# Remainder tiles moved to the beginning of a visit, and two pairs' loads moved to GpSimd's queue, in a fused cosine attention and two-layer MLP

## The chip, the cores and the metric

The kernel runs on one core of a Trainium2 chip. The metric is the device time of one execution in microseconds (us). The kernel before was run three times: 409.94 us in the median, 409.24 to 410.39. One more execution was profiled; it took 410.35 us, and its traced span is 408.6 us.

Engines are named as the profile names them: PE is TensorE (PEld its weight loads), DVE is VectorE, ACT is ScalarE, POOL is GpSimd, and SP is SyncE, which here only issues DMAs. DMAs issued by SP and those issued by GpSimd go through two different queues (q1 and q0 in the profile) to the same 16 DMA engines.

## The reference

Inputs are q, k and v, each 8 batches x 12 heads x 448 positions x 64 values in float32, tau = 0.1, and two weight matrices.

```
q_n = q / (norm(q, axis=-1) + 1e-6)
k_n = k / (norm(k, axis=-1) + 1e-6)
scores = q_n @ k_n.T / tau
attn = exp(scores - max) ; attn /= sum(attn) + 1e-9
x = (attn @ v) reordered to (8*448 tokens) x (12*64 = 768)
h = x @ w_in                  # 768 x 2048
g = max(0.01*h, h)
out = g @ w_out               # 2048 x 768
```

The output is 3584 x 768 in float32.

## The kernel before

**Units.** Two heads form a pair, so a batch has 6 pairs and the whole input 48 (numbered 0 to 47; pair s belongs to batch s // 6). The 448 positions are cut into three tiles of 128 and a remainder of 64. A pair's q and k lie in `raw_sb`, one of six slots (slot s % 6), so that loading pair s + 6 has to wait until pair s has been squared and normalised.

**Preparing a pair.** `load_qk(s)` (L134) issues four DMAs from SP: the main part of q, that of k, and the two remainders. `squares(s)` (L170) multiplies on GpSimd, `sums(s)` (L183) reduces on VectorE, `roots(s)` (L194) takes the square root on ScalarE as a logarithm and an exponential, `normalise(s)` (L210) adds the 1e-6, takes the reciprocal and multiplies q and k into `qn` on VectorE, and `transposes(s)` (L245) makes `qkT`, the transposed form. For the first ten pairs TensorE does the transposes and VectorE copies them out of PSUM; from pair 10 on (`DMA_FROM`) it is one transposing DMA issued from SP. `norm(s)` (L696) puts roots, normalise and transposes together, then issues the load of pair s + 4 (from pair 12 on; norm(11) loads 12 and 13), and then lets GpSimd square pair s + 2. Before it squares, GpSimd executes `hold`, a tiny copy that waits until `qn[s]` is written; all that GpSimd has after it waits too.

**Scores.** `key_tiles` (L264) takes a list of tiles. An ordinary tile (s, ki), ki from 0 to 2, is 128 keys of one pair against all 448 positions of both heads; a remainder tile (s, 3) holds the 64 remaining keys of two pairs, s - 1 and s, and so reads the transposed form of both. All matmuls of the list are issued first, each tile into two PSUM banks; then ScalarE takes the exponential of each tile. A batch has 18 ordinary tiles and 3 remainder tiles.

**Attend.** `attend_two` and `attend` (L656 to L683) sum the exponentials and multiply with v for four heads at a time (a j; three in a batch), ScalarE makes reciprocals of the sums, and `scale` on VectorE writes the result, transposed, to `xT`. `attend_batch(b)` does the three j of batch b. v and the weights are loaded by GpSimd's queue.

**The two layers.** Tokens are handled in eight chunks; chunk b has 384 tokens where b is even and 512 where it is odd, from the two batches of a pair of batches (batch 2m and 2m + 1). `firsts(b)` is layer one of chunk b: for 16 blocks m of 128 hidden columns, six matmuls each (kt = 0 to 5, 0.164 us apart with 384 columns), then the leaky ReLU on ScalarE. The first three blocks begin with kt 0 to 3 before kt 4 and 5 need the last attend's output. `groups` is layer two: for every 128 tokens 32 steps of two matmuls that run side by side, with the output row stored from SP.

**The order.** The order of work on each engine is written out by hand: an engine executes its instructions in the order of the program. One turn of the main loop is `visit(b)`, then `attend_batch(b + 1)`, then the loads of v for batch b + 2, then `firsts(b + 1)`. `visit(b)` (L725) is layer two of chunk b with the score tiles of batch b + 1 strewn in: the dictionaries `wide`, `three` and `four` say after which steps a tile comes, the first for all rows of 128 tokens but the last and the second for the last. Two remainder tiles come before the first step and the third after the last step. The argument `norms` hangs norm and sums calls on steps (row i, step n), and `between` in `firsts` hangs them on blocks m. Batches, chunks and visits are counted from 0.

**The beginning.** Pairs 0 to 5 are loaded at once by `load_first`, and their scores and attends run while the weights arrive. `bulk(s)` (L552) issues loads of v and w_in from GpSimd between pairs. Pairs 10 and 11 are loaded by SP behind explicit waits (`behind(...)`, L578 and L748). The four parts of w_out are loaded by GpSimd, the first after the third attend has written `xT` (L750 to L751) and the others in norm(6), norm(7) and norm(8). Visit 0 goes through two rows of 128 tokens at once in four parts, each part needing one of the four parts of w_out.

Of the kernel before, what the change touches and what calls it, by code (L numbers as in the profile page):

```python
# [16 lines left out]
def kernel(  # L17
# [37 lines left out]
    qtp = ctx.enter_context(tc.tile_pool(name="qt", bufs=5))  # L55
# [63 lines left out]
    def load_first(eng, x, part, s0, n):  # L119

        h0, i = 2 * s0, 0 if x is q else 1
        if part == 0:
            dst = raw_sb[:, s0 : s0 + n, :, 4 * i : 4 * i + 3]
            eng.dma_start(
                out=dst.rearrange("p s h t d -> p (s h) t d"), in_=main(x, 0, h0, 2 * n)
            )
        else:
            dst = raw_sb[64 * i : 64 * i + 64, s0 : s0 + n, :, 3]
            eng.dma_start(  # L129
                out=dst.rearrange("p s h d -> p (s h) d"),  # L130
                in_=x[0, h0 : h0 + 2 * n, MAIN:S].rearrange("h p d -> p h d"),
            )
# [340 lines left out]
    for part in range(2):  # L473
        load_first(nc.sync, q, part, 0, 1)
        load_first(nc.scalar, k, part, 0, 1)
    load_first(nc.sync, q, 0, 1, 1)
    load_first(nc.scalar, k, 0, 1, 1)
    for part, s, n in ((1, 1, 2), (0, 2, 1), (0, 3, 1), (0, 4, 1), (0, 5, 1)):
        for x in (q, k):
            load_first(nc.sync, x, part, s, n)  # L480
# [32 lines left out]
    for x in (q, k):  # L513
        load_first(gp, x, 1, 3, 3)
# [37 lines left out]
    def bulk(s):  # L552

        if s == 0:
            load_v(1)
            load_w_in(0, j=0)
        elif s == 1:
            load_v_rem(0, slice(2, 4))
            load_w_in(0, j=1)
        elif s == 2:  # L560
            load_w_in(0, j=2)
            load_v(2)
        elif s == 3:
            for e in range(2):
                load_w_in(1, e=e)

    def scaled(s):

        if s and s + 2 < NPAIR:
            sums(s + 2, (0,))  # L570
        normalise(s + 1)
        if s == 0:
            load_qk(7)
        elif s == 2:
            load_qk(8)
            load_qk(9)
        elif s == 4:
            behind(nc.sync, scalings[5], "weights first")  # L578
            load_qk(10)
        hold(qn[s + 1][:, 6, 0, 0:1])  # L580
        squares(s + 3)
        bulk(s)
        if s == 4:
            squares(8)
        if s + 2 < NPAIR:
            sums(s + 2, (1,))
# [67 lines left out]
    sums(8)  # L654
# [29 lines left out]

    def attend_batch(b):
        if b == 1:
            load_qk(14)
            load_qk(15)
            sums(12)
        attend_two(b * NQ)  # L690
        if b == 1:
            norm(12)
        attend(b * NQ + 2)


    def norm(s, transposed=True):  # L696
# [8 lines left out]
        for x in (12, 13) if s == 11 else (s + 4,) if s > 11 else ():  # L705
            load_qk(x)
# [18 lines left out]
    def visit(b, order, norms, between):  # L725
# [4 lines left out]
        key_tiles([(s0 + 1, 3), (s0 + 3, 3)])  # L730
        for i, pairs in enumerate(order):
            last = i == len(order) - 1
            after = between[last]
# [6 lines left out]
        key_tiles([(s0 + 5, 3)])  # L740

    three = ({5: 1, 11: 1, 16: 2, 21: 1, 27: 1}, {3: 1, 7: 1, 11: 1, 16: 2, 20: 1})
    wide = (dict.fromkeys((5, 11, 16, 22, 27, 33, 38, 44, 49, 55, 60), 1), {4: 1, 8: 1, 12: 1, 16: 2, 21: 1, 26: 1})
    four = ({5: 1, 11: 1, 16: 2, 24: 1}, {6: 1, 16: 2})
# [3 lines left out]
    behind(nc.sync, scalings[NQ - 1, 0], "weights first")  # L748
    load_qk(11)
    hold(xT[0][:, 2 * NQ - 2, 0:1])  # L750
    load_w_out((0,))  # L751
    norm(6, False)
    norm(7, False)
    firsts(
        0, SOON, {
            4: [lambda: norm(8, False)],
            5: [lambda: transposes(6), lambda: sums(9)],
            7: [lambda: transposes(7)],
            8: [lambda: norm(9, False)],
            10: [lambda: transposes(8), lambda: load_v(3)],  # L760
            11: [lambda: sums(10), lambda: load_v(4)],
            12: [lambda: transposes(9)],
            13: [lambda: norm(10), lambda: load_v(5), lambda: load_v_rem(1)],
# [3 lines left out]
    ready = 10  # L767
    for b in range(B):
# [9 lines left out]
        norms = {(0, 3): [lambda: norm(11)]}  # L778
        if b:
            norms = {}  # L780
            for i in range(tokens - 1):
                norms[i, 4] = [lambda s=ready + i: norm(s)]
                norms[i, 20] = [lambda s=ready + i + 1: sums(s)]
        visit(b, order, norms, wide if b == 0 else three if tokens == 3 else four)
        ready += tokens - 1
# [4 lines left out]
        s = ready  # L790
        between = {0: [lambda s=s: norm(s)], 1: [lambda s=s: sums(s + 1)]}
        if b == 0:
# [5 lines left out]
            ready += 4  # L798
        elif tokens == 3:
            between.update({  # L800
                4: [lambda s=s: norm(s + 1), lambda s=s: sums(s + 2)],
                7: [lambda s=s: norm(s + 2), lambda s=s: sums(s + 3)],
                10: [lambda s=s: norm(s + 3)], 13: [lambda s=s: sums(s + 4)],
            })
            ready += 4
        else:
            between.update({
                4: [lambda s=s: norm(s + 1)], 5: [lambda s=s: sums(s + 2)],
                8: [lambda s=s: norm(s + 2)], 12: [lambda s=s: sums(s + 3)],
            })  # L810
            ready += 3
# [36 lines left out]
```

## Time and profile before

| | us |
|---|---|
| median of three runs (lowest, highest) | 409.94 (409.24, 410.39) |
| the profiled execution | 410.35 |
| its span | 408.6 |
| TensorE matmul busy | 400.5 |
| ScalarE busy | 263.0 |
| VectorE busy | 189.8 |
| GpSimd busy | 139.7 |
| visit 0 begins | 52.1 |
| visit 2 begins | 147.4 |
| visit 4 begins | 242.1 |
| visit 6 begins | 336.8 |

A busy time is a sum over instructions; matmuls overlap and their ends are modelled, so a busy share of TensorE does not say that it runs at its peak. A timeline row gives the start and the length in us, the engine (SPq is SP's issuing of DMAs), the line, the operation with the tile written and the tile read, and how many instructions were merged; in brackets is the idle time of the engine before it and what ended that. A row of waits says who waited for whom: us in total, times, longest. Lines are those of the kernel before.

### The profile page before, as it was taken

How to read it: one execution, taken by the hardware profiler on the slowest of the kernel's cores; microseconds unless marked ns; L12 is line 12 of the kernel's file. 1: busy time of each engine (PE TensorE's matmuls, PEld its weight loads, DVE VectorE, ACT ScalarE, POOL GpSimd, SP SyncE). 2: the span in 40 equal slices, each digit the busy share in tenths (PEclk: the TensorE clock that was granted, in tenths of full speed). 3: DMA queues.
4: the chain of work that ended last, by engine and by line, in shares of the span. 5: the costliest groups of instructions: out<-in, count | busy, mean ns of one | idle time of the engine just before them, and what ended most of it. 6: DMA issues, size and time to landing. Idle time of an engine off the chain costs nothing.

```text
span 408.6 us, 10188 instructions
## 1 busy us (share of the span) xinstructions
PE 400.5 (98%) x4096; PEld 215.1 (53%) x4096; DVE 189.8 (46%) x405; ACT 263.0 (64%) x454; POOL 139.7 (34%) x214
## 2 busy tenths in 40 slices
PE   8998999999999999999999999999999999999996
PEld 3334556544555655544555555544555555544564
DVE  6887931761644724265552625257261645130021
ACT  5996488565866579745875569845776559944300
POOL 4983471481323433254241624055231530000000
PEclk9999999999999999999999999999999999999999
DMA  7999999697495939376386857486477732210033
GB/s 181 249 223 224 214 176 232 166 173 144 114 205 90 151 80 206 77 114 165 88 167 152 127 126 150 124 113 140 92 171 158 102 88 63 63 41 2 0 77 78
DMA packets 102111, 54.21 MB, mean 133 GB/s; under 512 B 70000, under 2 KB 97008, under 8 KB 102064
## 3 DMA queue, kind: packets, MB, share of 16 engines
q1 hardware_dynamic: 78064, 41.04, 43.6%
q0 software_dynamic: 23152, 12.00, 22.5%
q8 instruction: 32, 0.52, 0.5%
q10 hardware_dynamic: 848, 0.52, 0.4%
q14 instruction: 15, 0.12, 0.1%
HBM read 45.61 MB, written 11.01 MB: 139 GB/s over the span
## 4 chain that ended last, share of the span: by engine, by line
PE 86%; DMA 9%; POOL 2%; DVE 1%; issue 1%; ACT 0%; SPq 0%; POOLq 0%; DVEq 0%
PE ps L380 32%; PE ps L455 30%; PE ps L316 10%; PE ps L276 7%; DMA raw_sb<-in_k_dram 6%; PE ps L417 5%; DMA v_b<-in_v_dram 3%; POOL sq L179 1%; PE ps L303 1%; POOL v_rem L164 0%; DVE qn L219 0%; POOL w_in_sb L107 0%; POOL raw_sb L129 0%; ACT pe L288 0%; DVE xT L357 0%
## 5 line engine op out<-in xcount | busy, mean ns | idle before, releaser
L380 PE MATMUL ps<-xT,w_in_sb 128*128 128x384 bf16 (+1 forms) x768 | 147.9, 353 | 0.0
L455 PE MATMUL ps<-w_out_sb,hT 64*128 64x384 bf16 x1536 | 143.3, 323 | 0.0
L288 ACT ACTIVATE pe<-ps 128x896 bf16<-128x896 f32 x144 | 123.7, 918 | 19.8 <-PE ps L276 17.9
L387 ACT ACTIVATE hT<-ps 128x384 bf16<-128x384 f32 (+1 forms) x128 | 67.5, 543 | 72.7 <-PE ps L380 72.2
L380 PEld LDWEIGHTS <-w_in_sb 128*128 128x128 bf16 x768 | 74.0, 98 | 71.7 <-issue 3.7
L455 PEld LDWEIGHTS <-hT 64*128 64x128 bf16 x1536 | 74.9, 94 | 53.7 <-PE ps L455 4.0
L179 POOL TENSOR_TENSOR sq<-raw_sb 128x512 f32<-128x512 f32 x92 | 84.3, 936 | 21.1 <-DMA raw_sb<-in_k_dram 20.3
L219 DVE TENSOR_TENSOR qn<-raw_sb,r 128x512 bf16<-128x512 f32 x96 | 57.5, 640 | 1.6
L467 DVE COPY osb<-ps 128x384 f32<-128x384 f32 x41 | 21.2, 554 | 77.1 <-PE ps L455 46.6
L276 PE MATMUL ps<-qkT 64*128 64x448 bf16 (+1 forms) x384 | 54.7, 354 | 1.5 <-ACT pe L288 0.7
L190 DVE TENSOR_REDUCE ss<-sq 128x6 f32<-128x384 f32 (+1 forms) x95 | 54.4, 611 | 3.3 <-POOL sq L179 3.2
L510 POOL CAST seen<-qn 128x1 f32<-128x1 bf16 x47 | 8.9, 190 | 121.7 <-DVE qn L219 119.9
L214 DVE TENSOR_SCALAR ss<-ss 128x14 f32<-128x14 f32 x48 | 10.6, 222 | 66.2 <-ACT ss L198 66.2
L357 DVE TENSOR_TENSOR xT<-ps,rb 128x448 bf16<-128x448 f32 x48 | 27.9, 620 | 26.5 <-ACT rb L336 24.0
L157 POOL DMA_DIRECT2D v_b<-in_v_dram x24 | 18.5, 772 | 54.2 <-PE ps L316 54.2
L316 PE MATMUL ps<-pe,v_b 128*32 128x448 bf16 x576 | 32.0, 353 | 1.2 <-DMA v_b<-in_v_dram 1.2
L276 PEld LDWEIGHTS <-qkT 64*128 64x128 bf16 (+1 forms) x384 | 16.7, 96 | 21.1 <-issue 8.7
L316 PEld LDWEIGHTS <-v_b 128*32 128x32 bf16 x576 | 15.0, 97 | 13.4 <-DMA v_b<-in_v_dram 1.6
L423 DVE COPY osb<-ps 128x384 f32<-128x384 f32 (+1 forms) x9 | 4.6, 513 | 36.6 <-issue 22.6
L288 ACT ACTIVATE pr<-ps 128x896 bf16<-128x896 f32 x24 | 21.3, 921 | 0.2 <-PE ps L276 0.2
L335 ACT ACTIVATE rb<-ps 128x448 f32<-128x448 f32 x24 | 12.9, 538 | 13.2 <-PE ps L316 12.2
L417 PE MATMUL ps<-w_out_sb,hT 128*128 128x384 bf16 (+1 forms) x144 | 21.0, 308 | 0.0
(48 smaller groups left out, 186.5 us busy)
## 6 DMA issues: line engine op xcount, KB each, us to landing
raw_sb<-in_q_dram SPq DMA_DIRECT2D x48, 192.0 KB, 3.3
raw_sb<-in_k_dram SPq DMA_DIRECT2D x46, 192.0 KB, 3.4
out_dram<-osb SPq DMA_DIRECT2D x30, 192.0 KB, 2.9
v_b<-in_v_dram POOLq DMA_DIRECT2D x24, 192.0 KB, 4.9
out_dram<-osb SPq DMA_DIRECT2D x12, 384.0 KB, 2.9
w_out_sb<-in_moe_w_out_dram POOLq DMA_DIRECT2D x4, 768.0 KB, 10.4
w_in_sb<-in_moe_w_in_dram POOLq DMA_DIRECT2D x3, 512.0 KB, 9.3
w_in_sb<-in_moe_w_in_dram POOLq DMA_DIRECT2D x2, 768.0 KB, 15.2
```

Source lines behind the costliest of these rows:

```text
L179: eng.tensor_tensor(sq, x, x, op=ALU.mult)
L190: nc.vector.tensor_reduce(o.rearrange("p (h t) -> p h t", h=2), sqs[s][i], axis=AX.X, op=ALU.add)
L219: scalings[s] = nc.vector.tensor_tensor(qn[s][:, lo:hi], x.rearrange("p h t d -> p t h d"), r[:, r0 : r0 + 2 * nt].rearrange("p (h t) -> p ...
L276: nc.tensor.matmul(out=out[:, a, :S], lhsT=x[rows, c0:c1], rhs=x[rows, 0:S], start=True, stop=True,)
L288: nc.scalar.activation(out=dst, in_=sc[:, :, :S], func=AF.Exp, scale=inv_tau)
L316: nc.tensor.matmul(out=x[32 * g : 32 * g + 32, :S], lhsT=weights(g, ki) if ki < 3 else rem(g), rhs=pe[s][:, ki, a, :] if ki < 3 else pr[j] ...
L357: scalings[j, e] = nc.vector.tensor_tensor(xT[m][:, 2 * jj + e, half * S : (half + 1) * S], pos.pop((j, e))[:, :S], rbs[j], op=ALU.mult,)
L380: nc.tensor.matmul(out=pm[:, :n], lhsT=w_in_sb[:, kt, m * 128 : (m + 1) * 128], rhs=xT[c // 2][:, kt, c0 : c0 + n], start=(kt == 0), stop= ...
L387: nc.scalar.activation(out=hT[c][:, m, :n], in_=pms.pop((c, m))[:, :n], func=AF.Prelu, alpha=0.01)
L417: nc.tensor.matmul(out=po2[:, :n], lhsT=hT[c][:, m, ts * 128 : (ts + 1) * 128], rhs=w_out_sb[:, m, lo : lo + n], start=(m == 0), stop=(m = ...
L455: done[p][i] = nc.tensor.matmul(out=pos2[p][:, i, :HALF], lhsT=hT[c][rows, m, ts * 128 : (ts + 1) * 128], rhs=w_out_sb[rows, m, half * HAL ...
L467: copy(out=osb[c, ts][:, half * HALF : (half + 1) * HALF], in_=po2[:, i, :HALF])
```

## The change

There are five parts.

1. **Loads.** `load_first` becomes `load_pairs`, which can load several pairs of any batch. Pairs 10 and 11 are no longer loaded by SP behind waits; four DMAs on GpSimd's queue load both, issued in `scaled(4)` between squares(7) and squares(8), which puts them between the loads of w_in and those of w_out. The load of v for the third j comes ahead of the third w_in load in `bulk(2)`.
2. **Before visit 0.** roots(6) and normalise(6) come ahead of the third attend of batch 0, sums(8) later. The four TensorE transposes of pairs 6 to 9 are spread differently over layer one of chunk 0, and norm(11) moves from step 3 to step 18 of visit 0. The second part of w_out follows squares(9) directly.
3. **Remainder tiles.** From batch index 2 on, `visit` issues all three remainder tiles before its first step, so that all six pairs of the next batch have to be ready there. `qt` gets seven buffers instead of five.
4. **Preparing earlier.** The calls of norm and sums are placed anew. Layer one of chunk 2 now prepares four pairs (20 to 23), and the third attend of batch 2 has sums(19) and norm(19) ahead of it, those of batches 3 and 5 norm(25) and norm(37). norm(22) loads two pairs (26 and 27) and norm(23) two (28 and 29); from then on a norm loads the pair six further on, or, in layer one of chunks 3 and 5, four pairs are loaded together at block 11.
5. **Steps.** `wide`, `three` and `four` get other steps, now with one dictionary for each row of 128 tokens.

The diff, cut to its core:

```diff
-    qtp = ctx.enter_context(tc.tile_pool(name="qt", bufs=5))
+    qtp = ctx.enter_context(tc.tile_pool(name="qt", bufs=7))
...
         elif s == 2:
+            load_v(2)
             load_w_in(0, j=2)
-            load_v(2)
...
-        elif s == 4:
-            behind(nc.sync, scalings[5], "weights first")
-            load_qk(10)
...
         if s == 4:
+            for part in range(2):
+                for x in (q, k):
+                    load_pairs(gp, x, part, 10, 2)
             squares(8)
...
     sums(7)
-    sums(8)
+    roots(6)
+    normalise(6)
...
+    nexts = {1: 12, 2: 19, 3: 25, 5: 37}
...
         attend_two(b * NQ)
-        if b == 1:
-            norm(12)
+        if b == 2:
+            sums(19)
+        if b in nexts:
+            norm(nexts[b])
         attend(b * NQ + 2)
...
-    def norm(s, transposed=True):
+    def norm(s, transposed=True, load=True):
...
-        for x in (12, 13) if s == 11 else (s + 4,) if s > 11 else ():
+        after = {11: (12, 13), 22: (26, 27), 23: (28, 29)}
+        for x in after.get(s, () if s < 12 or not load else (s + (4 if s < 22 else NPAIR),)):
             load_qk(x)
...
-        key_tiles([(s0 + 1, 3), (s0 + 3, 3)])
+        key_tiles([(s0 + 1, 3), (s0 + 3, 3)] + [(s0 + 5, 3)] * (b > 1))
...
-        key_tiles([(s0 + 5, 3)])
+        if b < 2:
+            key_tiles([(s0 + 5, 3)])
...
+    wide = (at(8, 13, 18, 24, 29, 35, 40, 45, 50, 55, 60), at(4, 8, 12, 16, 16, 21, 26))
+    three = (at(9, 16, 16, 21, 26, 31), at(5, 10, 16, 16, 21, 26, 31), at(5, 10, 16, 16, 20))
+    four = (at(9, 16, 16, 24), at(4, 10, 16, 16, 24), at(4, 10, 16, 16, 24), at(5, 10, 16, 16))
...
-    behind(nc.sync, scalings[NQ - 1, 0], "weights first")
-    load_qk(11)
     hold(xT[0][:, 2 * NQ - 2, 0:1])
     load_w_out((0,))
-    norm(6, False)
+    hold(qn[6][:, 6, 0, 0:1])
+    squares(9)
+    load_w_out((4,))
     norm(7, False)
+    sums(8)
     firsts(
         0, SOON, {
+            3: [lambda: transposes(6)],
             4: [lambda: norm(8, False)],
-            5: [lambda: transposes(6), lambda: sums(9)],
-            7: [lambda: transposes(7)],
+            5: [lambda: sums(9), lambda: transposes(7)],
             8: [lambda: norm(9, False)],
-            10: [lambda: transposes(8), lambda: load_v(3)],
-            11: [lambda: sums(10), lambda: load_v(4)],
-            12: [lambda: transposes(9)],
-            13: [lambda: norm(10), lambda: load_v(5), lambda: load_v_rem(1)],
+            9: [lambda: transposes(8)],
+            10: [lambda: sums(10), lambda: load_v(3)],
+            12: [lambda: norm(10), lambda: load_v(4)],
+            13: [lambda: transposes(9), lambda: load_v(5), lambda: load_v_rem(1)],
             15: [lambda: sums(11)],
...
+        s = (b + 2) * NPAIR - (2 if b < 2 else 0)
+        if b == 0:
+            norms = {(0, 18): [lambda: norm(11)]}
+        elif b % 2:
             norms = {}
+            for i in range(3):
+                norms[i, 4] = [lambda x=s + i: norm(x)]
+                norms[i, 20] = [lambda x=s + i + 1: sums(x)] if s + i != 18 else []
+        else:
+            norms = {(2, 8): [lambda: sums(s + 1)], (2, 22): [lambda: norm(s)]}
...
+        elif b == 1:
+            between = {}
+            for x, m in zip(range(20, 24), (1, 4, 7, 10)):
+                between[m] = [lambda x=x: sums(x), lambda x=x: norm(x)]
+            between[14] = [lambda: sums(24)]
+        elif b % 2:
+            between = {
+                0: [lambda: norm(s + 3)], 2: [lambda: sums(s + 4)], 4: [lambda: norm(s + 4)],
+                6: [lambda: sums(s + 5)], 8: [lambda: norm(s + 5)], 12: [lambda: sums(s + 6)],
+            }
         else:
+            left = range(s + 2, s + NPAIR)
+            between = {}
+            for x, m in zip(left, (0, 3, 5, 8)):
+                between[m] = [lambda x=x: sums(x), lambda x=x: norm(x, load=False)]
+            between[11] = [lambda x=x: load_qk(x + NPAIR) for x in left]
+            between[14] = [lambda: sums(s + NPAIR)]
         firsts(b + 1, 0, between)
```

## The prediction

> **What bounds the kernel now.** I read the page first, then TensorE's waits, then the chain in order of time, then the timeline around two stretches. One profiled execution took 410.35 us: a span of 408.6 and 1.75 around it.
>
> ```profile
> PE 400.5 (98%) x4096; PEld 215.1 (53%) x4096; DVE 189.8 (46%) x405; ACT 263.0 (64%) x454; POOL 139.7 (34%) x214
> PE   8998999999999999999999999999999999999996
> ```
>
> From the third slice on TensorE is never free for long. Its list of waits, two lines of it:
>
> ```profile
> PE ps L316 <- DMA v_b<-in_v_dram: 1.2, 1, 1.2
> PE ps L276 <- ACT pe L288: 0.7, 3, 0.3
> ```
>
> The first is the third attend of batch 0, waiting for v; the second is spread over the first 57 us. After that the chain of the end is TensorE without a hole, and it repeats: visit 2 starts at 147.40, visit 4 at 242.10, visit 6 at 336.80, 94.70 us apart each. So the change can gain only before 57 us; later, anything that comes late is paid in full. The stretch that decides is layer one of batch 2 and the start of visit 2 (start, length, engine, line):
>
> ```profile
> 127.85 2.29 DVE L357 TENSOR_TENSOR xT<-ps,rb 128x448 bf16<-128x448 f32 x4 [2.37 <-ACT rb L336]
> ...
> 131.42 1.16 DVE L357 TENSOR_TENSOR xT<-ps,rb 128x448 bf16<-128x448 f32 x2 [1.28 <-ACT rb L336]
> ...
> 131.63 15.77 PE L380 MATMUL ps<-xT,w_in_sb 128*128 128x384 bf16 x96
> ...
> 138.65 1.26 SPq L251 DMA_TRANSPOSE qkT<-qn  x1
> ...
> 140.60 0.17 DVE L214 TENSOR_SCALAR ss<-ss 128x14 f32<-128x14 f32 x1 [1.20 <-ACT ss L198]
> ...
> 141.09 1.16 DVE L219 TENSOR_TENSOR qn<-raw_sb,r 128x512 bf16<-128x512 f32 x2
> ...
> 142.16 1.14 DVE L190 TENSOR_REDUCE ss<-sq 128x8 f32<-128x512 f32 x2
> 142.48 1.26 SPq L251 DMA_TRANSPOSE qkT<-qn  x1
> ...
> 147.33 0.57 PE L276 MATMUL ps<-qkT 64*64 64x448 bf16 x8
> ```
>
> Here three pairs are prepared in 15.7 us. A pair costs VectorE 1.14 (sums), 0.62 of waiting for ScalarE's roots and 1.65 (L214 to the end of L219): 3.4. On SP a transpose follows the end of L219 by 0.23, takes 1.26 to issue, and the four loads behind it end 3.83 after it began (138.65 to 142.48).
>
> **The change part by part.**
>
> *Start, up to 52 us.* v(2) goes ahead of a 512 KB w_in load. Totals end near 33.17 and the products began at 34.54: 1.37 gone. What is late next is xT. Normalise(6) (1.65 on VectorE, behind roots(6) at about 33.15) now stands ahead of the two scalings, sums(8) (1.1) behind them: they end near 36.0 instead of 36.9, so 1.0 is left. The transposes of pairs 6 to 9 have their inputs earlier; the gaps between 41.4 and 48.1 that now wait for them and for w_in (0.21, 0.07, 0.08, 0.25) are 0.5, and ScalarE's stall for roots(11) (56.12, 0.39 on TensorE) goes as norm(11) moves 15 steps later. With it transpose 11 is issued near 58.0 instead of 57.3 and the eight loads of pairs 12 and 13 behind it on SP 0.7 later; sums(12) is due at 72.9, the squares before it end near 72, so that hides too. Together 1.85, and I expect most of it not to last. Loads 10 and 11 leave SP (8 issues, two waits) for four GpSimd issues of about 0.8: squares(8) ends near 34 instead of 31.8, hidden, as sums(8) is needed only after 36.5. But their 917 KB now lie in the queue that brings w_out, ahead of all four parts. From issue and landing, w_out's parts now land at 48.0, 52.3, 56.1 and 61.6, and the last is first used at 62.45, a margin of 0.85. Without the other queue's traffic a 768 KB part takes about 3.8 (the quickest of them) instead of up to 4.8, 2.3 saved over four parts; the 917 KB cost 3.5 at the 260 GB/s that the load stretch after 75 us implies. So the last part lands between 61.1 and 62.8, while TensorE would be there at 60.6. I take -0.5 for the start; the ends are -1.85 (nothing waits) and +0.85 (62.8, and transpose 11 as slow as its 9.5 us now).
>
> *Attend of batch 2.* Sums(19) and norm(19) now stand between its scalings. VectorE: four scalings to 130.1, sums to 131.2, roots, normalise to 133.46, then the last two scalings to 133.9 and 134.5. ScalarE meanwhile stands at roots(19), ahead of the third reciprocal. TensorE has only 12 matmuls of 0.164 to cover it: free at 133.6, and waits 0.36 and 0.44: **+0.8** (0.6 to 1.1). In batches 3 and 5 norm alone is inserted, no sums, and 12 matmuls of 512 columns (2.6 us) cover it: nothing; if they did not, 0.5 each.
>
> *Layer one of batch 2, then visit 2.* Four pairs (20 to 23) are prepared in it, and the third remainder tile of visit 2, moved to its beginning, reads pairs 22 and 23. VectorE from 134.5: normalise(20) ends at 137.85, (21) at 141.15; GpSimd's squares(22) come behind seven v loads (4.8 us) and end at 142.3, so (22) ends at 145.15 and (23) at 148.45 (the v loads themselves end near 140 instead of 133, for use at 168). SP is slower still: transposes 20, 21, 22 at 138.1, 141.9, 145.8; then norm(22) issues the loads of **two** pairs, 26 and 27 (eight DMAs), before transpose 23: 145.8 + 3.83 + 2.4 = 152.0. It lands 3.0 later (the median in this stretch; 2.9 to 4.5), at 155.0. TensorE ends layer one at 147.34 + 0.8 = 148.2, does two remainder tiles (0.5) and stands at the third from 148.7: **+6.3**. Lower end 3.0, if SP's loads did not hold the transpose (148.45 + 0.23 + 3.0); upper end 7.8. ScalarE's leaky ReLUs, held back by roots(22) and (23) to about 149.7, lie inside the wait; with the wait gone they would cost 0.8.
>
> *The clock after it.* The first matmuls show what a TensorE does that comes from rest:
>
> ```profile
> 5.31 0.15 PEld L501 LDWEIGHTS <-warm 128*128 128x128 bf16 x1 [0.28 <-issue]
> ...
> 5.74 0.15 PEld L501 LDWEIGHTS <-warm 128*128 128x128 bf16 x1 [0.27 <-issue]
> ...
> 6.14 1.61 PEld L501 LDWEIGHTS <-warm 128*128 128x128 bf16 x8 [0.25 <-issue]
> ```
>
> One matmul of 512 columns each 0.43 us until 6.14, then each 0.20: half pace for 4.65 us from the first at 1.49, though the clock row shows full. After the wait of 1.19 at 34.54 the pace stayed full (18 L380 in 3.10). 6.3 us of rest is nearer the first than the second: half of 4.65, **+2.3**, ends 0 and 2.3.
>
> The Trainium skill ("TensorE: Matmul & The Clock Gate", What's actually happening) has the array fall to half rate after an idle window of about 3.4 us and recover after a busy one as long. By it the loss would be 1.7 and the sum below 8.0, not 8.6; the trace agrees on the half, and its 4.65 is longer.
>
> *Remainder tiles together.* Two at the start take 0.50 and one at the end 0.31; three together some 0.75: 0.06 in each of five visits, **-0.3** (0 to -0.3).
>
> *The rest.* In the three-token visits one norm is left instead of two, ScalarE's share falls, and TensorE waits for neither now. The sixteen load issues at step 11 of layer one in batches 3 and 5 (9.6 us of SP) end near 199.8, before the first store of the next visit. Batch 4's last transpose keeps the place that batch 2's third has now (142.48, landed by 145.5 for 147.4). The seven qt buffers cost no time. If this cover failed, a store or transpose would be a microsecond or two late.
>
> Sum: -0.5 + 0.8 + 6.3 + 2.3 - 0.3 = +8.6 on the profiled 410.35, 418.95. The median of the runs, 409.94, is 0.41 below that execution, so I predict **418.5**. A change of under 0.3% (1.2 us) could not be told from none.
>
> **Rivals.**
> - The wait, but no half pace: +6.3, **416.2**. For it: only rest before the program is shown to slow TensorE. Against: the length, five times that of the wait that left the pace full.
> - SP's loads do not hold transpose 23, and the wait stays 3.0, too short for the clock: -0.5 + 0.8 + 3.0 - 0.3 = +3.0, **412.9**. For it: the pair's normalise at 148.45 alone sets that. Against: now every transpose on SP begins only after the loads before it were issued.
> - Not slower: the third tile is not late. It decides at 148.7: transpose 23 must be issued by 145.7, which needs 2.7 us a pair on VectorE and no load in between. Then the wait and the clock go and -0.5 + 0.8 - 0.3 = 0.0 is left, **409.9**. For it: VectorE idles 0.62 a pair for the roots. Against: its instructions, sums, add, multiply, stand in the program's order throughout the trace.
> - The forecast with the start at its worst (w_out after the pairs, +0.85) and a landing of 4.5: 2.9 more, **421.4**.
>
> **How the numbers follow.** Forecast 0.55, no half pace 0.24, short wait 0.10, not slower 0.07, worse start 0.04. The forecast's own range is 416.5 to 420.5 (a start 1.35 better and a clock loss 0.6 smaller; a landing of 4.5 and a start 0.5 worse). Down to the short wait and its half microsecond, and up to the worse start, the range is 412.4 to 421.4. Faster 0.04 and same 0.03 split the not-slower case by the start's ends; slower 0.93.
>
> **What would show it.** In the changed profile: no wait of L316 for v_b near 33; TensorE waiting near 60 for a w_out load; two short waits of L380 for the xT scalings in batch 2; eight raw_sb issues on SP ahead of a transpose near 147 to 152, and the longest wait of TensorE, 5 to 7 us, ended by that transpose, with matmul pairs at twice their pace for some microseconds behind it; then 94.7 us from visit 4 to visit 6 again. The prediction is wrong if that transpose is issued before 146, or if TensorE goes on with L455 past the waiting tile (at 34.5 it did not pass its wait for v, with ready L380 work behind it).

## The result, and the profile after

The changed kernel takes 419.57 us in the median of six executions (418.59 to 420.93), the kernel before, with its further executions beside it, 409.59 us (408.99 to 413.14). The ratio is 1.0228, with a 95% interval of 1.0204 to 1.0251: 10.0 us slower, where 8.6 were forecast. The profiled execution of the changed kernel took 420.93 us with a span of 419.2, 10.6 more than the profiled one of before. Lines of code are three higher than before: L276 is now L279, L316 L319, L357 L360, L380 L383, L455 L458.

Where the 10.6 us arise is read from the same rows in both timelines (start in us):

| | before | after | later by |
|---|---|---|---|
| first attend of batch 1 | 72.56 | 73.36 | 0.80 |
| attend of batch 2 | 125.07 | 125.88 | 0.81 |
| layer one of batch 2 | 131.63 | 132.44 | 0.81 |
| visit 2, first score tile | 147.33 | 148.96 | 1.63 |
| visit 2, layer two | 147.84 | 158.07 | 10.23 |
| attend of batch 3 | 167.26 | 178.60 | 11.34 |
| attend of batch 7 | 356.66 | 367.29 | 10.63 |

So 0.8 come from the beginning, 0.8 between the attend of batch 2 and visit 2, 8.6 at the beginning of visit 2 and 1.1 in the rest of it; the four visits after that give back 0.7.

TensorE's list of waits in the changed kernel (engine, tile and line, who ended the wait: us in total, times, longest), its first six rows but the warm-up:

```profile
PE ps L279 <- DMA qkT<-qn: 5.8, 1, 5.8
...
PE ps L279 <- DVE qkT L260: 1.4, 3, 0.8
PE ps L236 <- DVE qn L222: 1.2, 2, 0.6
PE ps L383 <- DVE xT L360: 0.9, 4, 0.3
PE ps L279 <- ACT hT L390: 0.8, 1, 0.8
```

The wait for v is gone, no wait for w_out has come, and a single wait for a transposing DMA, 5.8 us, is larger than all others behind the warm-up together (5.0). The page's rows of TensorE and of its clock (tenths, 40 slices) show it in the fifteenth slice, from 146.7 us, where TensorE was full before:

```profile
PE   8999999999999939999999999999999999999996
...
PEclk9999999999999988999999999999999999999999
```

The timeline of the same place (start, length, engine, line, tiles, number; in brackets the wait and who ended it):

```profile
144.12 1.53 SPq L254 DMA_TRANSPOSE qkT<-qn  x1
...
148.28 1.26 SPq L254 DMA_TRANSPOSE qkT<-qn  x1
...
148.96 0.37 PE L279 MATMUL ps<-qkT 64*64 64x448 bf16 x1
149.64 0.53 SPq L142 DMA_DIRECT2D raw_sb<-in_q_dram  x1
150.17 1.61 PE L279 MATMUL ps<-qkT 64*64 64x448 bf16 x9 [0.83 <-ACT hT L390]
...
153.88 0.60 SPq L145 DMA_DIRECT2D raw_sb<-in_k_dram  x1
154.59 1.26 SPq L254 DMA_TRANSPOSE qkT<-qn  x1
...
157.55 0.58 PE L279 MATMUL ps<-qkT 64*64 64x448 bf16 x2 [5.78 <-DMA qkT<-qn]
...
158.07 3.06 PE L458 MATMUL ps<-w_out_sb,hT 64*128 64x384 bf16 x18
```

Normalise(23) ended at 151.70, but SP was issuing the eight loads of pairs 26 and 27 one behind the other from 149.64 to 154.48; only then came transpose 23, which landed 2.92 later, and the third remainder tile went at 157.55. And the clock, in stretches of 2 us (the column behind the five engines' busy times is the granted clock):

```profile
152.00:154.00 2.00, 0.00 (x0) 0.00 (x0) 0.75 (x2) 1.64 (x3) 1.83 (x3) 1.00 0.68 173
154.00:156.00 2.00, 0.00 (x0) 0.00 (x0) 0.00 (x0) 0.00 (x0) 0.00 (x0) 0.54 0.66 188
156.00:158.00 2.00, 0.45 (x2) 0.12 (x2) 0.00 (x0) 0.00 (x0) 0.00 (x0) 0.50 0.85 185
158.00:160.00 2.00, 2.00 (x16) 0.91 (x16) 0.00 (x0) 0.92 (x1) 0.00 (x0) 0.50 0.57 159
160.00:162.00 2.00, 2.00 (x22) 1.06 (x20) 0.00 (x0) 0.64 (x1) 0.00 (x0) 0.75 0.70 212
162.00:164.00 2.00, 2.00 (x28) 1.09 (x25) 0.00 (x0) 1.59 (x3) 0.00 (x0) 1.00 0.04 9
```

From 154.2 to 161.0 TensorE is granted half its clock: 16 matmuls in 2 us, then 28.

### The profile page after: what moved, and what is told of

It reads as the page before. It is cut to its first block, busy times and chain, and to the rows that moved or that the text cites. A ratio compares the mean times of both kernels' runs of the same rounds, so it can differ in the third digit from the quotient of the medians.

```text
span 419.2 us, 10163 instructions
## 1 busy us (share of the span) xinstructions
PE 402.9 (96%) x4096; PEld 226.2 (54%) x4096; DVE 200.8 (48%) x405; ACT 261.7 (62%) x454; POOL 144.2 (34%) x218
## 4 chain that ended last, share of the span: by engine, by line
PE 84%; DVE 10%; ACT 3%; issue 1%; DMA 1%; SPq 0%; POOL 0%; POOLq 0%; DVEq 0%
PE ps L458 30%; PE ps L383 28%; PE ps L319 9%; PE ps L279 8%; PE ps L420 5%; DVE qn L222 4%; PE ps L504 2%; DVE ss L193 2%; PE ps L306 1%; DVE xT L360 1%; DVE ss L217 1%; ACT pe L291 1%; DVE qkT L260 1%; ACT ss L200 1%; DMA qkT<-qn 1%
## 5 line engine op out<-in xcount | busy, mean ns | idle before, releaser
L383 PE MATMUL ps<-xT,w_in_sb 128*128 128x384 bf16 (+1 forms) x768 | 148.5, 353 | 0.9 <-DVE xT L360 0.9
L458 PE MATMUL ps<-w_out_sb,hT 64*128 64x384 bf16 x1536 | 145.4, 325 | 0.0
L291 ACT ACTIVATE pe<-ps 128x896 bf16<-128x896 f32 x144 | 125.0, 918 | 21.8 <-PE ps L279 20.2
L383 PEld LDWEIGHTS <-w_in_sb 128*128 128x128 bf16 x768 | 74.1, 98 | 73.0 <-issue 5.5
L458 PEld LDWEIGHTS <-hT 64*128 64x128 bf16 x1536 | 84.6, 95 | 45.8 <-PE ps L458 4.5
L390 ACT ACTIVATE hT<-ps 128x384 bf16<-128x384 f32 (+1 forms) x128 | 65.0, 541 | 48.0 <-PE ps L383 47.2
L182 POOL TENSOR_TENSOR sq<-raw_sb 128x512 f32<-128x512 f32 x92 | 86.5, 963 | 12.1 <-DMA raw_sb<-in_k_dram 11.2
L470 DVE COPY osb<-ps 128x384 f32<-128x384 f32 x41 | 21.2, 552 | 94.9 <-PE ps L458 58.3
L222 DVE TENSOR_TENSOR qn<-raw_sb,r 128x512 bf16<-128x512 f32 x96 | 64.5, 713 | 1.8 <-DMA qkT<-qn 0.2
L279 PE MATMUL ps<-qkT 64*128 64x448 bf16 (+1 forms) x384 | 56.7, 354 | 8.9 <-DMA qkT<-qn 5.8
L217 DVE TENSOR_SCALAR ss<-ss 128x14 f32<-128x14 f32 x48 | 14.4, 300 | 60.5 <-ACT ss L201 60.2
L200 ACT ACTIVATE ss<-ss,tiny 128x14 f32<-128x14 f32 x48 | 14.6, 305 | 35.3 <-DVE ss L193 34.9
L360 DVE TENSOR_TENSOR xT<-ps,rb 128x448 bf16<-128x448 f32 x48 | 27.7, 618 | 15.4 <-ACT rb L339 15.3
L279 PEld LDWEIGHTS <-qkT 64*128 64x128 bf16 (+1 forms) x384 | 18.2, 97 | 27.0 <-issue 8.9
L319 PE MATMUL ps<-pe,v_b 128*32 128x448 bf16 x576 | 32.0, 353 | 0.0
L319 PEld LDWEIGHTS <-v_b 128*32 128x32 bf16 x576 | 15.2, 97 | 11.9 <-issue 0.6
```

Of the source, the lines that this page charges most:

```text
L182: eng.tensor_tensor(sq, x, x, op=ALU.mult)
L222: scalings[s] = nc.vector.tensor_tensor(qn[s][:, lo:hi], x.rearrange("p h t d -> p t h d"), r[:, r0 : r0 + 2 * nt].rearrange("p (h t) -> p ...
L279: nc.tensor.matmul(out=out[:, a, :S], lhsT=x[rows, c0:c1], rhs=x[rows, 0:S], start=True, stop=True,)
L291: nc.scalar.activation(out=dst, in_=sc[:, :, :S], func=AF.Exp, scale=inv_tau)
L319: nc.tensor.matmul(out=x[32 * g : 32 * g + 32, :S], lhsT=weights(g, ki) if ki < 3 else rem(g), rhs=pe[s][:, ki, a, :] if ki < 3 else pr[j] ...
L360: scalings[j, e] = nc.vector.tensor_tensor(xT[m][:, 2 * jj + e, half * S : (half + 1) * S], pos.pop((j, e))[:, :S], rbs[j], op=ALU.mult,)
```

## The experiments

All are made from the changed kernel unless said otherwise, and each ratio is against the kernel before on the same chip (medians there 410.25, 409.59 and 409.98 us for the three groups: the first four, the next four and the last three).

### 1. Transpose 23 ahead of the loads

```diff
-        after = {11: (12, 13), 22: (26, 27), 23: (28, 29)}
+        after = {11: (12, 13), 22: (), 23: (26, 27, 28, 29)}
```

> The changed kernel, but the loads of pairs 26 and 27 are issued behind transpose 23 instead of ahead of it. Theory (SP's order sets when transpose 23 starts): it is issued when its pair is normalised, near 152.0 instead of 154.6, lands near 155.0, TensorE's longest wait falls from 5.8 to 3.2 us, and the run from 419.6 to about 417 (416 if the shorter rest also spares part of the half pace). Rival (the landing is set by DMA traffic, not by the order on SP): transpose 23 lands at 157 as before and the time stays at 419.6.

Measured: 417.70 us (415.78 to 418.55), ratio 1.0178 [1.0141, 1.0215]. Two rows of its timeline, transposes 22 and 23 on SP (merged in one row) and the tile:

```profile
145.98 4.88 SPq L254 DMA_TRANSPOSE qkT<-qn  x2
...
152.58 0.58 PE L279 MATMUL ps<-qkT 64*64 64x448 bf16 x2 [3.08 <-DMA qkT<-qn]
```

The wait is 3.08 instead of 5.78: SP's eight loads were worth 2.7 us of it, and what is left is set by normalise(23) (148.41 to 149.57) and a landing of 2.9. In the ratios the total fell by some 2 us, but the four executions lie 2.8 us apart. The two profiled executions differ by 3.8, and 2.0 of that is the beginning (first attend of batch 1 at 71.36 instead of 73.36). So the other order on SP brought some 1.8 us, less than the wait became shorter, since the clock fell here too:

```profile
150.00:152.00 2.00, 0.00 (x0) 0.00 (x0) 0.63 (x2) 1.46 (x2) 1.73 (x2) 0.86 0.59 114
152.00:154.00 2.00, 1.42 (x8) 0.55 (x10) 0.00 (x0) 0.80 (x1) 0.00 (x0) 0.50 0.77 208
154.00:156.00 2.00, 2.00 (x16) 0.94 (x14) 0.00 (x0) 0.12 (x1) 0.00 (x0) 0.50 0.70 199
156.00:158.00 2.00, 2.00 (x16) 0.92 (x14) 0.00 (x0) 0.92 (x1) 0.00 (x0) 0.50 0.61 153
158.00:160.00 2.00, 2.00 (x26) 1.05 (x24) 0.00 (x0) 1.19 (x2) 0.00 (x0) 0.94 0.59 165
```

By stretches of 0.5 us, it was half from 151.4 to 158.3, 6.8 us as in the changed kernel (154.2 to 161.0). But here TensorE was at work again 1.2 us after the fall (152.58), there 3.4 us after it, so more of the half-clock time was work: the first 32 layer-two matmuls took 5.33 us (153.09 to 158.42) against 2.80 at full clock (experiment 3), a loss of 2.5, against 1.4 in the changed kernel. The shorter wait gave 1.1 of its gain back to the clock.

### 2. The third tile of visit 2 at the end

```diff
-        key_tiles([(s0 + 1, 3), (s0 + 3, 3)] + [(s0 + 5, 3)] * (b > 1))
+        key_tiles([(s0 + 1, 3), (s0 + 3, 3)] + [(s0 + 5, 3)] * (b > 2))
...
-        if b < 2:
+        if b < 3:
             key_tiles([(s0 + 5, 3)])
```

> The changed kernel, but visit 2 has its third remainder tile at the end, as in the kernel before; visits 3 to 6 keep all three at the beginning. Theory (the tile's place in visit 2 costs the whole wait and the clock after it): layer two of visit 2 begins near 150.5 instead of 158.1, the granted clock stays at 1.0, and the run takes 411 to 412.5; what is left over 409.6 is the start (+0.8), the attend of batch 2 (+0.8) and up to 1 us in which ScalarE, held back by roots(23), catches up. Rival (ScalarE's backlog of leaky ReLUs is the true bound there, and the transpose only hides it): layer two begins later than 153 and the run stays above 414.

Measured: 412.58 us (412.25 to 412.81), ratio 1.0054 [1.0035, 1.0073]. The tile's place in this one visit, with the clock that falls behind it, is 7.0 of the 10.0 us in the medians. In this kernel the clock stays at 1.00 there (144 to 156), and layer two of visit 2 starts at 149.39. Its list of waits shows what is left and what is new:

```profile
PE ps L306 <- DVE osb L470: 1.3, 1, 1.3
PE ps L383 <- DVE xT L360: 0.9, 4, 0.3
...
PE ps L279 <- ACT hT L390: 0.7, 1, 0.7
```

New is the first: the last copy of an output row (L470) stands on VectorE behind normalise(24), hung at step 22 of the last row, and the attend of batch 3 waits for its PSUM. In the changed kernel that copy is as late (180.33, after the attend's begin at 178.60), but TensorE doesn't wait for it; why is not shown. The third row is the leaky ReLUs of layer one, held back by the roots: visit 2's first tile goes at 147.22 and its layer two 2.17 later, where before it was 0.51, so 1.7 us that the long wait had covered. The rows add up to nearly the same as the medians. Tile and clock were 8.3 (158.07 less 148.96 less 2.17 is 6.9, and the clock 1.4). Less the 1.3 that is new, and less 0.3 for the tile at its old place, 6.7 are left, beside 7.0.

### 3. Unused matmuls while the tile waits

```diff
-        key_tiles([(s0 + 1, 3), (s0 + 3, 3)] + [(s0 + 5, 3)] * (b > 1))
+        key_tiles([(s0 + 1, 3), (s0 + 3, 3)] + [(s0 + 5, 3)] * (b > 2))
+        if b == 2:
+            fill(24)
+            key_tiles([(s0 + 5, 3)])
```

> The changed kernel, with 24 idle-filling matmuls of 512 columns (about 5.2 us, their result is not used) between the second and the third remainder tile of visit 2. Theory (TensorE falls to half pace because it rests): the third tile still comes at about 157.5, the granted clock stays at 1.0 behind it, the first nine steps of layer two take 1.5 us instead of 3.0, and the run takes about 418.2, 1.4 less. Rival (those steps are slow because their hT blocks come late from ScalarE): they stay at 3.0 and the run at 419.6 or, with the fill running over, above.

Measured: 417.39 us (417.24 to 417.61), ratio 1.0177 [1.0153, 1.0201]. Its timeline:

```profile
149.39 5.13 PE L504 MATMUL ps<-warm 128*128 128x512 bf16 x23 [0.16 <-issue]
...
155.46 0.38 PE L279 MATMUL ps<-qkT 64*64 64x448 bf16 x2 [0.64 <-DMA qkT<-qn]
...
155.77 1.64 PE L458 MATMUL ps<-w_out_sb,hT 64*128 64x384 bf16 x18
```

The granted clock is 1.00 in every stretch from 148 to 164, and 18 layer-two matmuls take 1.64 us where they took 3.06 in the changed kernel. So the half pace is the rest's doing, and it is worth the 1.4 us between these rows. The other 0.8 of the 2.2 in the medians is no gain of the filling. The beginning ran otherwise (first attend of batch 1 at 71.42 in the profiled execution, 73.36 in that of the changed kernel), which the next experiments explain.

### 4. The beginning alone

The kernel before with the change's beginning: v(2) ahead, roots and normalise(6) early, pairs 10 and 11 through GpSimd, the steps of `firsts(0)`, norm(11) at step 18. From visit 1 on everything is as before:

```diff
-    nexts = {1: 12, 2: 19, 3: 25, 5: 37}
+    nexts = {1: 12}
...
-        if b == 2:
-            sums(19)
...
-        after = {11: (12, 13), 22: (26, 27), 23: (28, 29)}
+        after = {11: (12, 13)}
...
-        key_tiles([(s0 + 1, 3), (s0 + 3, 3)] + [(s0 + 5, 3)] * (b > 1))
+        key_tiles([(s0 + 1, 3), (s0 + 3, 3)])
...
-        if b < 2:
-            key_tiles([(s0 + 5, 3)])
+        key_tiles([(s0 + 5, 3)])
```

> The kernel before, with only what the change does up to visit 0: the loads of pairs 10 and 11 on GpSimd's queue, v ahead of the third w_in load, normalise(6) ahead of the third attend, the new places of the transposes of pairs 6 to 9, norm(11) at step 18, the new steps of visit 0, seven qt buffers. Theory (VectorE's order: the copy of transpose 9 stands behind normalise(10), so the second remainder tile waits 0.8): the first attend of batch 1 begins near 73.4 instead of 72.6 and the run takes 410.4, 0.8 more than before. Rival (the start as predicted, the rest of the change costs it): 409.1, 0.5 less than before.

Measured: 409.79 us in ten executions, ratio 1.0000 [0.9983, 1.0018]: no gain and no loss. But the ten lie apart: six from 408.96 to 410.11, four from 410.78 to 411.40. The profiled one is the highest of them, and its visit 0 begins layer two late, at 54.14. So does the profiled one of the changed kernel, the highest of its six, at 53.94 (before: 52.62; in experiments 1 to 3: 51.93 to 52.19). The difference is on VectorE. First the changed kernel, then the one of experiment 2, the same normalise(9) and squares(11):

```profile
45.89 3.29 DVE L222 TENSOR_TENSOR qn<-raw_sb,r 128x512 bf16<-128x512 f32 x2
...
46.46 2.31 POOL L182 TENSOR_TENSOR sq<-raw_sb 128x512 f32<-128x512 f32 x2
```

```profile
45.79 1.47 DVE L222 TENSOR_TENSOR qn<-raw_sb,r 128x512 bf16<-128x512 f32 x2
...
47.26 1.82 POOL L182 TENSOR_TENSOR sq<-raw_sb 128x512 f32<-128x512 f32 x2
```

Two multiplies of VectorE take 1.16 us alone and 3.29 when GpSimd's squares run into them. The Trainium skill ("SBUF — State Buffer", sections "SBUF: two separate sides" and "Who interferes with whom") says that a VectorE instruction with both inputs in SBUF and a GpSimd instruction that reads SBUF lock each other out, the one that comes second standing still for the whole instruction of the other; the trace agrees (1.16 against 3.29, and 1.82 against 2.31 for GpSimd). What it costs follows in the kernel of this experiment:

```profile
49.44 0.34 PE L236 MATMUL ps<-id,qn 128*128 128x128 bf16 x3 [0.66 <-DVE qn L222]
...
53.15 0.62 DVE L260 COPY qkT<-ps 128x896 bf16<-128x896 bf16 x1
...
53.83 0.38 PE L279 MATMUL ps<-qkT 64*64 64x448 bf16 x4 [0.81 <-DVE qkT L260]
```

Transpose 9 waits 0.66 for normalise(9), its copy then comes on VectorE behind normalise(10) (52.08 to 53.24), and the second remainder tile of visit 0 waits 0.81 for the copy. When squares(11) come depends on when the loads of pairs 10 and 11 land: squares(10), ahead of them, waited for its load until 43.73 in the changed kernel and until 44.41 in experiment 2, whose beginning is the same.

### 5. Sums(19) back in visit 1

Experiment 2's kernel, and in it

```diff
-        if b == 2:
-            sums(19)
...
-                norms[i, 20] = [lambda x=s + i + 1: sums(x)] if s + i != 18 else []
+                norms[i, 20] = [lambda x=s + i + 1: sums(x)]
```

> As the run with the third remainder tile of visit 2 at the end, and sums(19) back in visit 1 (row 2, step 20), as in the kernel before; only norm(19) stays ahead of the third attend of batch 2. Theory (sums and norm together make the last two scalings late): the two waits of layer one of chunk 2 for xT (0.3 and 0.2 in the list, 0.8 on the chain) go, the time falls by 0.8 to 411.8. Rival (the 0.8 is ScalarE's: roots(19) ahead of the third reciprocal costs it, sums or not): 412.6 as before.

Measured: 411.12 us (410.60 to 412.79), ratio 1.0041 [1.0014, 1.0068]. The wait of layer one for `xT` fell from 0.9 us in four to 0.4 in two, the two that are left being those of batch 0: sums(19) made the waits of batch 2. From the attend of batch 2 to visit 2 it is 22.27 us (125.69 to 147.96), where it was 23.08 in the changed kernel and 22.26 before. In the total it can't be told from experiment 2 (the intervals overlap): its seven executions again lie in two groups, four from 410.60 to 411.12 and three from 412.56 to 412.79.

### 6. Another order for the beginning, with the rest mended

From experiment 2's kernel. The beginning: normalise(6) behind the third attend as before, transposes 6 to 9 at steps 5, 7, 10 and 13, norm(10) at 14. The rest: sums(19) in visit 1; layer one of batch 2 prepares only pairs 20 to 22; norm(23) and norm(24) hang in visit 2, whose tiles keep the steps of before. Visits 3 to 6 keep their three tiles at the beginning.

```diff
-    roots(6)
-    normalise(6)
...
-    hold(qn[6][:, 6, 0, 0:1])
-    squares(9)
-    load_w_out((4,))
+    norm(6, False)
...
+            if b == 2:
+                norms = {
+                    (0, 4): [lambda: norm(23)], (0, 20): [lambda: sums(24)],
+                    (1, 4): [lambda: norm(24)], (1, 20): [lambda: sums(25)],
+                }
...
-            for x, m in zip(range(20, 24), (1, 4, 7, 10)):
-                between[m] = [lambda x=x: sums(x), lambda x=x: norm(x)]
-            between[14] = [lambda: sums(24)]
+            between = {
+                0: [lambda: sums(20)], 1: [lambda: norm(20), lambda: sums(21)], 4: [lambda: norm(21)],
+                5: [lambda: sums(22)], 8: [lambda: norm(22)], 12: [lambda: sums(23)],
+            }
```

> A version meant to beat both: the change's loads at the start, but normalise(6) behind the third attend, transposes 6 to 9 at blocks 5, 7, 10, 13 and norm(10) behind transpose 9; sums(19) in visit 1; pairs 20 to 22 prepared in layer one of chunk 2, norm(23) and norm(24) in visit 2 with its third remainder tile at the end and the steps of before; visits 3 to 6 as in the change. Theory (what the change costs is the order around transposes 9 and 23; what it brings is the v wait, 1.2, and 0.15 to 0.2 in each visit with three tiles at its beginning): no wait of TensorE above 0.7 us behind 35 us, 407.9, 2 under before. Rival (the start's gain is given back to w_out's loads, and the visits' gain is the steps', not the tiles'): 409.5 or more.

Measured: 409.82 us (409.28 to 411.69), ratio 1.0012 [0.9997, 1.0027]: a miss. All the waits near visit 2 are gone, but transpose 9 now waits 1.4 us for normalise(9). VectorE comes to it 1.0 us later than in experiment 2 (45.74 against 44.71), and its first step (L217, 0.17 us alone) takes 1.50 while GpSimd issues a load and begins squares(11). The twelve executions again lie in two groups, eight from 409.28 to 410.16 and four from 411.32 to 411.69.

### 7. That beginning alone

Experiment 4's kernel with the beginning of experiment 6.

> The kernel before with the change's start alone, and that start mended as in the run beside it (normalise(6) behind the third attend, transposes 6 to 9 at blocks 5, 7, 10, 13, norm(10) behind transpose 9). Theory (the start alone was even in the median because in a part of the executions normalise(9) meets GpSimd's squares(11), takes 3.3 instead of 1.5 us and makes the copy of transpose 9 miss its place): the executions no longer fall in two groups 1.8 us apart, and the time is 408.6, 1.3 under before. Rival (the two groups come from the order in which the loads land, whatever VectorE's order): they remain, 409.8.

Measured: 410.54 us (408.48 to 412.48), ratio 1.0020 [1.0002, 1.0039]. A miss too: another order of the copies on VectorE does not take the spread away, which is 4.0 us from end to end here. But the meeting itself was not taken away either: in the profiled execution the first step of normalise(9) takes 1.87 us (45.90 to 47.77) beside squares(11), which began at 46.65, and transpose 9 waits 1.7.

### 8. The rest alone

The beginning of the kernel before, and from visit 1 on experiment 6's kernel.

> The kernel before up to visit 0, and from visit 1 on the version meant to beat both. Theory: start and rest add up, so the rest alone gives 0.7, 409.3, and the starts of visits 4 and 6 lie 94.4 us or less apart instead of 94.7. Rival (three tiles at the beginning save nothing by themselves): 94.7 and 410.

Measured: 409.42 us (407.93 to 411.48), ratio 0.9994 [0.9976, 1.0011], which tells nothing. Its profile does: from the attend of batch 5 to that of batch 7 are 94.35 us (261.40 to 355.75), before 94.70 (261.96 to 356.66), and in the changed kernel 94.35 too. So visits 3 to 6 as the change has them are worth 0.17 us each. Of this the tiles explain 0.11: three together take 0.70, where two and one took 0.50 and 0.31. The rest is not placed, since the steps and the norms of these visits are other ones too.

### 9. Squares(11) out of normalise(9)'s way

Experiment 4's kernel; squares(11) and the last part of w_out go from norm(8) to norm(9), where GpSimd first waits for `qn[9]`:

```diff
-        if s != 9:
+        if s != 8:
             squares(s + (3 if s < 9 else 2))
-        if s < 9:
-            load_w_out((4 * (s - 5),))
+        if s in (7, 9):
+            load_w_out((8 if s == 7 else 12,))
```

> The kernel before with the change's start alone, and in it GpSimd's squares(11) and the last w_out load moved from norm(8) to norm(9), behind the hold on qn[9]. Theory (a normalise that meets squares on GpSimd stands still until they end; squares(11) starts in the middle of normalise(9) in a part of the executions): normalise(9) takes 1.5 us or less in every execution, the copy of transpose 9 keeps its place, no run is above 410.2, and the median is 409.3, 0.5 below the start alone. Rival (the spread of 2.4 us between executions is set by when the loads land): the spread and 409.8 remain.

Measured: 409.42 us in twelve executions, ratio 0.9975 [0.9957, 0.9993], the highest 409.83: the upper group, four of ten in experiment 4, is gone. Its timeline:

```profile
43.65 1.16 DVE L222 TENSOR_TENSOR qn<-raw_sb,r 128x512 bf16<-128x512 f32 x2
...
47.58 1.82 POOL L182 TENSOR_TENSOR sq<-raw_sb 128x512 f32<-128x512 f32 x2
...
50.68 0.72 PE L279 MATMUL ps<-qkT 64*64 64x448 bf16 x8
```

Normalise(9) is at its 1.16 us again, and visit 0's remainder tiles go at 50.68 (before: 52.12). The profiles of the other executions with this beginning fit: normalise(9) took 3.29 or 3.30 us in the changed kernel, experiment 4 and experiment 5, each time in a late execution, and 1.46 or 1.47 in experiments 1 to 3. So this meeting made the two groups. Only one execution of each kernel was profiled, and the last w_out load moved along with squares(11); no list shows a wait of TensorE for it.

### 10. Squares(9) out of normalise(7)'s way as well

```diff
-    hold(qn[6][:, 6, 0, 0:1])
-    squares(9)
     load_w_out((4,))
...
+        if s == 7:
+            squares(9)
```

> As the run beside it, and squares(9) also behind the hold on qn[7] instead of qn[6], so that it no longer meets normalise(7) (3.1 us in the changed kernel instead of 1.2). Theory (same lock): TensorE's wait of 0.6 for qn at transpose 7 goes, 408.7. Rival (squares(9) then meets normalise(8) and the wait only moves): 409.3.

Measured: 408.71 us (408.43 to 409.33), ratio 0.9957 [0.9939, 0.9975]. Here the beginning gains 0.4% where experiment 4 gained nothing. A smaller meeting is left, of squares(10) and normalise(9) (2.00 us instead of 1.16); no wait of TensorE shows it.

### 11. Both mends together

The beginning of experiment 10 and the rest of experiment 6.

> The start of the run beside it and, from visit 1 on, the version whose visits 3 to 6 have three remainder tiles at their beginning and visit 2 its third at the end. Theory: 0.7 under that run, 408.0, and 1.5 under the kernel before. Rival (the start's gain is not there): 409.0 or more.

Measured: 407.87 us (407.55 to 408.20), ratio 0.9935 [0.9912, 0.9959], 2.1 us below the kernel before on that chip, and the best version here. Its list of TensorE's waits, without the warm-up, in full down to 0.4 us:

```profile
PE ps L279 <- DVE qkT L260: 0.6, 2, 0.3
PE ps L279 <- ACT pe L291: 0.5, 2, 0.3
PE ps L383 <- DVE xT L360: 0.4, 2, 0.2
```

## Why the prediction was right, and where it was off

The forecast was 418.5 in a range of 412.4 to 421.4; the median is 419.57. The mechanism that carried the sum was right, and three of its terms were off, partly against each other.

- **Third tile, +6.3: right in kind, measured 8.1.** TensorE was ready for it at 149.5 (148.96 and 0.5 for two tiles), and it went at 157.55. Expected for transpose 23 was 152.0, issued it was at 154.59. Of the 2.6, 0.8 are the beginning, which moved both sides. The other 1.8 were lost on two engines at once. On SP the four loads behind transpose 19 took 4.2 us to issue instead of the 2.4 that I took (one of them 2.43, beside GpSimd's v loads; why is not shown), which put transpose 20 1.1 later than its normalise allowed. On VectorE normalise(21) ran into GpSimd's squares(22), as normalise(9) does in experiment 4:

```profile
141.19 2.36 POOL L182 TENSOR_TENSOR sq<-raw_sb 128x512 f32<-128x512 f32 x2
...
141.49 2.48 DVE L222 TENSOR_TENSOR qn<-raw_sb,r 128x512 bf16<-128x512 f32 x2
```

  Its two multiplies took 2.48 us instead of 1.16, and it ended at 143.97, just when SP came free (144.01); normalise(22) and SP met again at 148.10 and 148.12. In experiments 1 and 2 SP was free 0.3 and 0.8 us before normalise(21) ended, so by these rows VectorE alone makes the transposes as late, and quicker issues on SP would have gained next to nothing; no run tries it. The working has neither loss, though its own times already let squares(22), to 142.3, overlap normalise(21), to 141.15. The landing was 2.92 against 3.0. The term's upper end, 7.8, was too low for the same reasons. The lower end, 3.0, looks like the wait of 3.08 in experiment 1, but that is chance: from TensorE's being ready to the tile it is 5.1 us there (147.46 to 152.58), with the wait for the ReLUs in it, since normalise(23) ended 2.1 us after TensorE was ready and not 0.25 before.
- **The leaky ReLUs inside the wait: right**, and so was that they would cost once the wait was gone, but 0.8 was too little: 1.7 in experiment 2.
- **The clock, +2.3: it fell, but measured 1.4.** The rival without half pace is out by the clock's rows and by experiment 3. The mis-sized part was how much of the half-clock time would be work: I took half of 4.65 us. It recovered 3.5 us after TensorE was back, and 1.7, the estimate from the Trainium skill's window of 3.4 us ("TensorE: Matmul & The Clock Gate", What's actually happening), was nearer than mine; in experiment 1 the same fall cost 2.5, so no single number holds.
- **Attend of batch 2, +0.8: right**, 0.82 from the attend to visit 2. Only 0.5 of it stands in named waits (0.29 and 0.21), the rest in gaps too short to be listed. Experiment 5 shows sums(19) as the cause.
- **Tiles together, -0.3: the sign right, the size 0.7.** Each of visits 3 to 6 is 0.15 to 0.20 shorter, not 0.06; the tiles themselves explain 0.11 of it (experiment 8).
- **The beginning, -0.5: wrong in its working.** The step that failed is the one on w_out: its last part landed at 58.9 (issued at 48.72, 10.2 later), 2.2 ahead of the earliest time that I gave, and no wait for it came. What came instead, GpSimd's squares standing in VectorE's normalise, is nowhere in the working; squares(9) and (11) were moved, and I asked only whether they came in time, not what they ran beside. The kernel before shows such a meeting already, of squares(9) and normalise(7):

```profile
39.12 2.27 POOL L179 TENSOR_TENSOR sq<-raw_sb 128x512 f32<-128x512 f32 x2
39.18 2.63 DVE L219 TENSOR_TENSOR qn<-raw_sb,r 128x512 bf16<-128x512 f32 x2
```

  The result is +0.8 in the profiled execution, about -1.0 in others (first attend of batch 1 at 71.4 to 71.6 against 72.56), and 0.0 in the median of experiment 4.
- **The rival "SP's loads do not hold transpose 23"** falls with experiment 1, in which moving them away took 2.7 us off the wait; "not late at all" falls with the timeline.

By the measured sizes: 0.8 for the beginning, 0.8 for the attend, 8.6 for the beginning of visit 2 (8.1 of standing and 0.5 for the tile itself), 1.1 for the rest of that visit (1.4 of clock less 0.3 for the tile that is no longer at its end), -0.7 for the visits after: 10.6, the difference of the two profiled executions.

## What to carry to other kernels

When a consumer is moved forward, follow its last input through every queue on the way: here the late normalise alone made TensorE wait 3.1 us (experiment 1), and eight prefetch loads in front of one transposing DMA made that 5.8, though the first of what they loaded was not read by GpSimd before 180.75, 26 us later. A stall that lets TensorE's clock fall is paid a second time, and shortening the stall alone can raise that second payment; taking the tile back, or filling the stall, got rid of it. And when work of GpSimd is moved in time, look at which instructions of VectorE it now runs beside, the multiplies of two inputs above all, not only at whether it is done in time.

## What the hardware showed that was not expected

- **Half clock in pieces of one length.** In the changed kernel and in experiment 1 the clock was half for 6.8 us both times, though the waits were 5.8 and 3.1 us long, and it fell 2.4 and 1.9 us after the last matmul's end. Between the start of visit 2 and the fall TensorE had been busy only in part, and a wait of 3.1 us was enough. 6.8 is twice the 3.4 us window of the Trainium skill ("TensorE: Matmul & The Clock Gate", What's actually happening), which it calls free-running; both lengths agree with that, but no run here varied the phase.
- **The lock makes a kernel's times fall into groups.** The 0.8 us by which squares(11) come earlier or later (46.46 against 47.26) decide between 3.29 and 1.47 us for normalise(9), and that between visit 0's layer two at 53.94 and at about 52.1. Letting GpSimd's squares(9) and (11) wait for the normalise they collided with took the groups away and with them 0.4% of the time (experiments 4 and 10). Executions of the kernel before lie up to 4.1 us apart as well (409.37 to 413.47 on the chip of experiments 9 to 11); whether its own meeting of squares(9) and normalise(7) makes that was not tested.
- **A step of one input is stretched too.** L217, 0.17 us alone, took 0.85 at 140.33 in the changed kernel and ended 0.05 us after GpSimd had issued its v loads (138.65 to 141.13). In experiments 1 and 2 it ended 0.05 after them as well; that they hold it is inferred from these ends alone.
- **SP's issue times are not constant.** Loads of the same kind were issued in 0.41 to 0.65 us in most rows and once in 2.43; the same load took 1.84 in experiment 1 and 1.07 in experiment 2.
